# Four tiles of attention: the values product turned round, and one add of the weight decoding moved from GpSimd to VectorE

## The chip, the cores and the metric

The kernel runs on one core of a Trainium2 chip. The metric is the device time of one execution in microseconds (us); the median of several runs counts. A core has five engines that take their instructions in order: TensorE (PE, with PEld for its weight loads), VectorE (DVE), ScalarE (ACT), GpSimd (POOL) and SyncE (SP), which here issues every DMA.

## What is computed

Attention that keeps the 32 largest scores of each row, over 4 batches of 8 heads, 576 tokens and 64 columns; then an MLP with h * cos(h); then eight experts, all of them applied to all 2304 tokens and weighted by a matrix P that is normalised by rows and columns eight times.

```python
scores = scale * q @ k.T
mask = scores >= kth_largest(scores, 32)
attn = exp(where(mask, scores, -1e9) - max)
attn = attn / (attn.sum(-1) + 1e-9)
x = (attn @ v) as [2304, 512]
h = x @ w_in            # [512, 2048]
x2 = (h * cos(h)) @ w_out
P = exp(x2 @ w_gate - max)   # 8 rounds of row and column normalising
out = sum over e of P[:, e] * (relu(x2 @ w1[e]) @ w2[e])
```

`w_in` and `w_out` come in float64, all else in float32.

## The kernel before, in words

Every instruction is noted by `put` (or `dma`) in program order with what it reads and writes. `Plan.issue` then simulates the engines with estimated costs and picks, per engine, the ready instruction of lowest priority number; the order that results is fixed in each engine's queue. The priorities depend on the class of work: first attention, first MLP, decode, attention, other MLP. On DVE the first MLP (0) goes ahead of decode (0.5), which goes ahead of the first attention (1); on POOL and ACT the first attention (0) goes ahead of decode (1).

**Decode** (`decode`, lines 314 to 333) turns 32 blocks of [128, 512] float64 weights into float32 and writes them to DRAM: one DMA in, a shift on DVE (line 324), four passes on ACT (325 to 328), a product on POOL (329), a mask on DVE (330), a product on POOL (331), the last add on POOL (332), and one DMA out. Its buffers are rings of four or five. The 16 blocks of `w_in` come first, then the 16 of `w_out`.

**The opening** handles the first 512 tokens in four tiles of 128, in float32 products. `attention_tile` goes over 8 heads in pairs. For each head `att_tile` makes the scores on PE (line 450, two halves, evicted by ACT at 456), finds the 32nd largest on DVE (`max` and `match_replace`, 458, 463, 464), takes the exponential on ACT (460), masks it and sums the rows in one DVE instruction (465), adds 1e-9 to the sums on POOL (467), takes the reciprocal on DVE (468) and scales the row by it on POOL (469). PE transposes the row in five pieces (474), ACT evicts them to `at_f` (478). In `attention_tile` the function `av` then multiplies, with the values stationary and the probabilities moving, into 64 partitions of the PSUM bank `ps_t` (529), and ACT copies that to half a chunk of `x_f` (533), which thus holds the features on the partitions.

`moe1_tile_a` multiplies `x_f` by the decoded `w_in` (629), chunk by chunk of `x_f`, in two alternating banks; `gate` makes h * cos(h) (587 to 596, POOL, DVE and ACT); PE transposes it (638) and ACT evicts it to `gT` (641). `moe1_tile_b` multiplies by the decoded `w_out` (654) in one bank, transposes (661) and splits x2 into two float32r parts (668, 669). The program order is tile 0, tile 1, MLP a of 0, tile 2, MLP a of 1, MLP b of 0, and so on.

**After the opening**, from x2 of the first 512 tokens on, `fill` runs the experts on them (mm3, lines 371 to 373) beside the attention of the other tokens (`attention`, whose values product is at 500 and 502). Buffers of `fill` take the place of the first tiles' (pool `fl` after `first`), those of `attention` the place of decode's (`att` after `dec`). The rest of the first MLP and the experts of the other tokens follow.

Of the kernel before, what the change touches and what calls it, by code (L numbers as in the profile page):

```python
# [24 lines left out]
# priorities per engine (lower first) of: attention of the first tokens, their first MLP,  # L25
# the decoding of weights, attention of the other tokens, the other MLP work
# [10 lines left out]
class Buf:  # L37
    """A tile that is allocated when the first instruction on it is issued."""
# [13 lines left out]
class View:  # L52
    """A slice of a Buf's first free dimension"""
# [17 lines left out]
class Plan:  # L71
    """Instructions are noted in program order with what they read and write; `issue` orders
    them per engine (greedy, by priority, on estimated costs) and then issues them."""
# [156 lines left out]
def fused_kernel(tc, kq, vv, w_in, w_out, w_gate, w1, w2, out, B=4):  # L230
    """Every product of two float32 operands a*b is carried by float32r parts:
    a = ah + al and b = bh + bl, each part exact in float32r, and
    ah*bh + ah*bl + al*bh accumulates in float32."""
# [7 lines left out]
    NMAX = 320  # queries of an attention product  # L241
    # the tokens' cut, in tiles of 128: those whose second MLP runs beside the attention, one half
    # of them at a time, those whose first product there goes by Winograd's scheme, the rest
# [42 lines left out]
    # PSUM, a bank each  # L286
# [27 lines left out]
    def decode(src, keep, part):  # L314
        """float64 bits to the nearest float32; what is under 2**-126 becomes zero.
        With h and l the high and low words, the float32 of sign, exponent and the 20 high
        mantissa bits comes from h alone (11 exponent bits to 8: the low 8, the top one of
        them flipped), and l, scaled by the exponent, is added to it."""
        raw, mag, sgn, low = d_raw(), d_mag(), d_sgn(), d_low()
        dma(lambda: raw.ap, lambda: src.bitcast(I32), 1 << 19, writes=[raw])  # L320
        hi = lambda dt: raw.ap.bitcast(dt).rearrange("p (n t) -> p n t", t=2)[:, :, 1]
        lo = lambda: raw.ap.bitcast(U32).rearrange("p (n t) -> p n t", t=2)[:, :, 0]
        magf = lambda: mag.ap.bitcast(F32)
        put("DVE", 335, lambda: V.tensor_scalar(mag.ap, hi(I32), 3, 0x40000000, op0=ALU.logical_shift_left, op1=ALU.bitwise_xor), [raw], [mag])
        put("ACT", 613, lambda: A_.activation(sgn.ap, hi(F32), AF.Identity, bias=cols.ap[:, 1:2]), [raw, cols], [sgn])
        put("ACT", 613, lambda: A_.activation(sgn.ap, sgn.ap, AF.Sign, bias=cols.ap[:, 2:3]), [sgn, cols], [sgn])
        put("ACT", 520, lambda: A_.activation(low.ap, lo(), AF.Copy, scale=2.0**-52), [raw], [low])
        put("ACT", 520, lambda: A_.activation(magf(), magf(), AF.Abs), [mag], [mag])
        put("POOL", 1225, lambda: G_.tensor_tensor(magf(), magf(), sgn.ap, op=ALU.mult), [mag, sgn], [mag])
        put("DVE", 335, lambda: V.tensor_scalar(sgn.ap.bitcast(I32), mag.ap, -8388608, None, op0=ALU.bitwise_and), [mag], [sgn])  # L330
        put("POOL", 1225, lambda: G_.tensor_tensor(low.ap, low.ap, sgn.ap, op=ALU.mult), [low, sgn], [low])
        put("POOL", 1225, lambda: G_.tensor_tensor(low.ap, magf(), low.ap, op=ALU.add), [mag, low], [low])
        dma(keep, lambda: low.ap, 1 << 18, [low], [part])
# [7 lines left out]
    def split_cols(hi, lo, raw, n=512, eng="POOL"):  # L341
        """raw, hi, lo: (buffer, view) pairs; eng takes the low parts"""
        (rb, rv), (hb, hv), (lb, lv) = raw, hi, lo
        put("ACT", act_ns(n), lambda: A_.activation(hv(), rv(), AF.Copy), [rb], [hb])  # L344
        e, f, c = ("POOL", G_, pool_ns(n)) if eng == "POOL" else ("DVE", V, dve_ns(n))
        put(e, c, lambda: f.tensor_tensor(lv(), rv(), hv().bitcast(F32), op=ALU.subtract), [rb, hb], [lb])  # L346

    # who takes the first MLP's low parts of weights, ranges of hs, low parts of gates
# [28 lines left out]
    def mm12(o, ob, ah, al, bh, bl, n, start, stop, bufs):  # L377
        """mm3 in two steps, of which only the second needs bl"""
# [30 lines left out]
    at_r = ring_of("first", 2, [128, 5, 128], F32, "at_f")  # L409
    xf_r = ring_of("first", 2, [128, 4, 128], F32, "x_f")  # L410
# [24 lines left out]
    def att_tile(stats, dests, plain=None):  # L435
        """stats: (stationary q buffer, first column, head), whose scores add up to the tile's
        128 rows. dests: (first row, rows, head, first token column) of the tile. plain: the
        tile's operands where it goes by float32 products."""
# [30 lines left out]
        put("POOL", 724, lambda: G_.tensor_scalar(ex.ap, ex.ap, mc(35), 0.0, op0=ALU.mult, op1=ALU.add), [ex, (m, 35, 36)], [ex])  # L469
        pt = lambda: ps_t.ap.rearrange("p (c t) -> p c t", c=4)  # L470
        for c0, c1, p in ((0, 4, 128), (4, 5, 64)):
# [8 lines left out]
            for r0, rn, hd, t0 in dests:  # L480
# [3 lines left out]
                if c0:  # L484
                    # the low parts of the last 64 keys lie below the high ones
# [7 lines left out]
                put("DVE", dve_ns(k), lambda hv=hv, sv=sv, lv=lv: V.tensor_tensor(lv(), sv(), hv().bitcast(F32), op=ALU.subtract), [ps_t, hi], [lo])  # L493

# [15 lines left out]
    def attention_tile(t):  # L510
        """Tokens t * 128.. of the first batch, all heads, in float32 products"""
        nonlocal work
        work = "first attention"
        x_f, q = xf_r(), qp_r()
        s0 = t * 128
        dma(lambda: q.ap, lambda: kq[0:H, 0:64, 1, s0 : s0 + 128].rearrange("h d s -> d h s"), 1 << 18, writes=[q], slow=True)
        for pr in range(H // 2):
# [3 lines left out]
            dma(lambda v=v: v.ap, lambda hs=hs: vv[hs].rearrange("h p c d -> p h c d"), 128 * 2560, writes=[v])  # L521
            for j in range(2):
                at_f = at_r()
                att_tile([], [], dict(q=q, k=k, at=at_f, h=2 * pr + j))

                def av(v=v, j=j, at_f=at_f):
                    for c in range(5):
                        p = 64 if c == 4 else 128
                        T_.matmul(ps_t.ap[:64, :128], v.ap[:p, j, c, :], at_f.ap[:p, c, :], start=c == 0, stop=c == 4)

                put("PE", 1100.0, av, [v, at_f], [ps_t])
                r = slice(64 * j, 64 * j + 64)
                put("ACT", act_ns(128, psum=True), lambda pr=pr, r=r: A_.activation(x_f.ap[r, pr, :], ps_t.ap[:64, :128], AF.Copy), [ps_t], [(x_f, pr, pr + 1)])
# [37 lines left out]
    def load_cols(src, h, l, c0, t0, n):  # L571
        """Columns t0.. of src [128, 4, NT] as parts, to columns c0.. of h and l"""
# [8 lines left out]
    def gate(hs, rr, n=1024):  # L581
        """rr = hs * cos(hs), n columns; hs, rr: (buffer interval, view) pairs"""
# [31 lines left out]
    def moe1_tile_a(t, x_f):  # L614
        """hs * cos(hs) of 128 tokens, transposed; float32 products with the tokens stationary"""
# [60 lines left out]
    class Part:  # L676
        """A block of tokens in the first MLP: where its x, h, y, gates and x2 are"""
# [10 lines left out]
        # of the sums that share a bank, the first matmul opens the group and the last closes it  # L688
# [61 lines left out]
    def keep_raw(xb, i0):  # L750
        """x2 in float32 to slots i0.. of xb"""
# [14 lines left out]
    def keep_parts(h2, l2):  # L766
        """x2 as parts"""
# [14 lines left out]
    def gates(v, vb, n, g_r, psum):  # L782
        """relu(v) as parts"""
# [5 lines left out]
    def fill(e, t0, h_ring):  # L789
        """Expert e on the four tiles from t0, whose x2 is in x2fh and x2fl, not yet weighted"""  # L790
# [63 lines left out]
    # The first product of the second MLP by Winograd's form of Strassen's scheme, exact in  # L854
    # real arithmetic: with W1^T in blocks A and x2^T in blocks B (rows of A: the halves of F;
    # columns of A, rows of B: the halves of the model dimension; columns of B: halves of the
    # tokens), seven products of blocks give the four blocks C of W1^T x2^T.
    #   S1 = A21 + A22, S2 = S1 - A11, S3 = A11 - A21, S4 = A12 - S2
    #   T1 = B12 - B11, T2 = B22 - T1, T3 = B22 - B12, T4 = B21 - T2
    #   U = A11 B11 + S2 T2, V = U + S3 T3, W = S1 T1  # L860
    #   C11 = A11 B11 + A12 B21, C12 = U + W + S4 B22, C21 = V + A22 T4, C22 = V + W
# [3 lines left out]
    def combine(x2, th, tl):  # L865
        """The right operands from x2's four row blocks, slots 0-3 the first half of the
        tokens, 4-7 the second"""
# [11 lines left out]
    def weight_mix(e, j, wa_r, mix_r):  # L879
        """The left operands for F's chunks j and j + 4, as (hi, lo) chunks of two each"""  # L880
# [18 lines left out]
    def mixed_first(A, th, tl, mix_r, g_r):  # L899
        """The parts of relu of two chunks of F by both halves of the tokens"""  # L900
# [84 lines left out]
    def sum_fill():  # L985
        """The weighted sums of what `fill` kept, a term a step"""
# [29 lines left out]
    # the first 512 tokens: a tile at a time, so that the tensor engine has work early  # L1016
# [16 lines left out]
    # beside the attention of the other batches: the second MLP of 1024 tokens  # L1033
# [12 lines left out]
    # the first MLP of the others, and their second  # L1046
# [78 lines left out]
```

## Time and profile before

| | us |
|---|---|
| median of 3 runs | 2483.45 (2482.08 to 2484.89) |
| span of the profiled execution | 2483.0 |
| PE busy in it | 2390.7 (96%) |
| VectorE busy | 1929.3 (78%) |
| ScalarE busy | 1261.6 (51%) |
| GpSimd busy | 1258.1 (51%) |

No time of the profiled execution is given but its span, which runs from its first instruction to the end of its last. Busy shares are means over stages with different limits; the stretches have to be read one by one. "Granted clock" is the share of TensorE's full clock that it was given.

### The profile page before, as it was taken

Reading aid. Unit: us, or ns where it says so; the run is one execution under the profiler, and the core shown is the slowest. Engines: PE = TensorE matmul, PEld = TensorE weight load, DVE = VectorE, ACT = ScalarE, POOL = GpSimd, SP = SyncE. Lnnn points to the kernel's source line nnn. Section 1 sums busy time; section 2 is a strip of 40 time slices with the busy share of each in tenths; the row PEclk is TensorE's granted clock in tenths of the full one; section 3 lists DMA queues with packets and bytes.
Section 4 is the critical chain, followed back from the end, with each engine's and each line's share of the span. In section 5 each row is a group of like instructions: output and inputs, shape, how many; then the busy total and the mean of one; then the engine's idle time right before and its main releaser. Section 6 shows DMA issues by size and latency. Waiting matters only on the chain.

```text
span 2483.0 us, 33670 instructions
## 1 busy us (share of the span) xinstructions
PE 2390.7 (96%) x11261; PEld 1866.3 (75%) x11261; DVE 1929.3 (78%) x3570; ACT 1261.6 (51%) x2430; POOL 1258.1 (51%) x1332
## 2 busy tenths in 40 slices
PE   6889999999999889999999999989999999999999
PEld 3444568888777767878778878867888888888887
DVE  8999559999999999999961567577667676666665
ACT  6786556666666776666543666552232232232221
POOL 6886257566666776665544120264334334453440
PEclk8679999999999999999999999999999999999999
DMA  8776664344334333333333432212223223111111
GB/s 266 228 219 187 198 202 146 100 118 119 113 118 124 95 91 99 119 114 100 92 112 118 136 103 64 69 39 59 85 77 98 81 81 95 46 48 38 34 39 43
DMA packets 156606, 267.81 MB, mean 108 GB/s; under 512 B 15680, under 2 KB 54176, under 8 KB 156432
## 3 DMA queue, kind: packets, MB, share of 16 engines
q1 hardware_dynamic: 156432, 265.66, 35.5%
q8 instruction: 88, 1.44, 0.3%
q14 instruction: 86, 0.70, 0.1%
HBM read 231.90 MB, written 33.70 MB: 107 GB/s over the span
## 4 chain that ended last, share of the span: by engine, by line
PE 56%; DVE 22%; POOL 3%; ACT 2%; issue 2%; DMA 1%; SPq 0%; POOLq 0%; ACTq 0%; DVEq 0%
PE y L371 8%; PE y L373 8%; PE y L372 8%; DVE wk L463 5%; DVE m L464 5%; DVE ex L465 3%; PE g L373 2%; PE g L371 2%; PE g L372 2%; DVE gl L786 2%; PE h L371 2%; PE h L373 2%; PE h L372 2%; DVE atl L493 1%; DVE m L458 1%
## 5 line engine op out<-in xcount | busy, mean ns | idle before, releaser
L346 POOL TENSOR_TENSOR wlo<-raw,whi 128x512 fp32r<-128x512 f32 x320 | 429.0, 1343 | 266.5 <-ACT whi L344 219.1
L464 DVE MAX8 m<-wk 128x8 f32<-128x576 f32 x432 | 317.2, 748 | 2.1
L344 ACT ACTIVATE whi<-raw 128x512 fp32r<-128x512 f32 x376 | 235.0, 627 | 122.9 <-PE y L373 32.1
L980 DVE SCALAR_TENSOR_TENSOR acc<-y,P,acc 128x512 f32<-128x512 f32 x280 | 209.0, 747 | 86.8 <-PE y L373 85.9
L463 DVE MATCH_REPLACE8 wk<-m,wk 128x576 f32<-128x576 f32 x288 | 213.4, 742 | 1.2
L371 PE MATMUL y<-whi,gh 128*128 128x512 f32 x512 | 206.0, 402 | 0.0
L373 PE MATMUL y<-whi,gl 128*128 128x512 f32 x512 | 201.1, 393 | 0.0
L372 PE MATMUL y<-wlo,gh 128*128 128x512 f32 x512 | 200.7, 392 | 0.0
L456 ACT ACTIVATE sc<-s 128x288 f32<-128x288 f32 x288 | 117.3, 407 | 120.9 <-DVE ex L465 60.2
L474 PE MATMUL t<-ident,ex 128*128 128x128 f32 (+1 forms) x720 | 136.5, 290 | 31.1 <-DVE atl L493 7.0
L474 PEld LDWEIGHTS t<-ident,ex 128*128 128x128 f32 (+1 forms) x720 | 87.2, 141 | 102.8 <-issue 21.1
L465 DVE SCALAR_TENSOR_TENSOR ex<-sc,m,ex 128x576 f32<-128x576 f32 x144 | 157.2, 1092 | 1.5
L371 PE MATMUL y<-gh,xh 128*128 128x512 f32 x362 | 141.5, 391 | 0.0
L373 PE MATMUL y<-gh,xl 128*128 128x512 f32 x362 | 141.1, 390 | 0.0
L372 PE MATMUL y<-gl,xh 128*128 128x512 f32 x362 | 141.1, 390 | 0.0
L469 POOL TENSOR_SCALAR ex<-ex,m 128x576 f32<-128x576 f32 x144 | 113.2, 786 | 47.0 <-DVE m L468 43.1
L460 ACT ACTIVATE ex<-sc,m 128x576 f32<-128x576 f32 x144 | 111.5, 774 | 39.0 <-POOL m L459 37.6
L458 DVE MAX8 m<-sc 128x8 f32<-128x576 f32 x144 | 106.9, 743 | 20.6 <-ACT sc L456 20.6
L492 ACT ACTIVATE ath<-t 128x512 fp32r<-128x512 f32 (+3 forms) x256 | 97.6, 394 | 46.2 <-PE t L474 41.4
L373 PEld LDWEIGHTS y<-whi,gl 128*128 128x128 f32 x512 | 96.1, 188 | 21.5
L371 PE MATMUL y<-gh,gh 128*128 128x512 f32 x278 | 109.1, 392 | 3.2 <-ACT gh L785 2.1
L346 POOL TENSOR_TENSOR cl<-raw,ch 128x512 fp32r<-128x512 f32 x32 | 43.4, 1365 | 132.9 <-ACT ch L344 132.9
(420 smaller groups left out, 7156.6 us busy)
## 6 DMA issues: line engine op xcount, KB each, us to landing
raw<-in_w_dram SPq DMA_DIRECT2D x384, 256.0 KB, 2.7
kq<-in_kq_dram SPq DMA_DIRECT2D x32, 576.0 KB, 4.1
wp<-win_d SPq DMA_DIRECT2D x32, 512.0 KB, 4.4
wp<-wout_d SPq DMA_DIRECT2D x32, 512.0 KB, 4.3
y_d<-st SPq DMA_DIRECT2D x64, 256.0 KB, 2.6
raw<-y_d SPq DMA_DIRECT2D x64, 256.0 KB, 2.7
raw<-win_d SPq DMA_DIRECT2D x48, 256.0 KB, 3.0
raw<-wout_d SPq DMA_DIRECT2D x48, 256.0 KB, 2.7
```

Source lines behind the costliest of these rows:

```text
L344: put("ACT", act_ns(n), lambda: A_.activation(hv(), rv(), AF.Copy), [rb], [hb])
L346: put(e, c, lambda: f.tensor_tensor(lv(), rv(), hv().bitcast(F32), op=ALU.subtract), [rb, hb], [lb])
L371: T_.matmul(o(), ah(), bh(), start=start, stop=False)
L372: T_.matmul(o(), ah(), bl(), start=False, stop=False)
L373: T_.matmul(o(), al(), bh(), start=False, stop=stop)
L456: put("ACT", act_ns(288, psum=True), lambda c=c: A_.activation(sc.ap[:, c], o(), AF.Copy), [ps_s], [(sc, c.start, c.stop)])
L458: put("DVE", 669, lambda: V.max(mc(0, 8), sc.ap), [sc], [(m, 0, 8)])
L463: put("DVE", 669, lambda r=r, src=src: V.match_replace(wk.ap, mc(8 * r, 8), src.ap, LOWEST), [src, (m, 8 * r, 8 * r + 8)], [wk])
L464: put("DVE", 669, lambda r=r: V.max(mc(8 * r + 8, 8), wk.ap), [wk], [(m, 8 * r + 8, 8 * r + 16)])
L465: put("DVE", 729, lambda: V.scalar_tensor_tensor(ex.ap, sc.ap, mc(31), ex.ap, op0=ALU.is_ge, op1=ALU.mult, accum_out=mc(33)), [sc, ex, (m, ...
L474: T_.transpose(pt()[:p, c - c0, :], ex.ap[:, c * 128 : c * 128 + p], ident.ap)
L980: put("DVE", 663, lambda y=y, av=av, pcol=pcol: V.scalar_tensor_tensor(av(), y.ap, pcol(), av(), op0=ALU.mult, op1=ALU.add), [y, P, a], [a])
```

## The change

Only the functions below change; comments and docstrings are also taken out, which moves no instruction. In decode the last add goes to DVE, at the planner's cost for that engine. In the first four tiles, line 469 is left out; the product puts the tokens on the output partitions, with the probabilities stationary and the values moving, each head in its own 64 columns of the bank `ps_g`; ACT's eviction to the new buffer `x_t` multiplies by the reciprocal of the row sums; after the eighth head four transposes and one eviction make `x_f`.

```diff
-        put("POOL", 1225, lambda: G_.tensor_tensor(low.ap, magf(), low.ap, op=ALU.add), [mag, low], [low])
+        put("DVE", dve_ns(512), lambda: V.tensor_tensor(low.ap, magf(), low.ap, op=ALU.add), [mag, low], [low])
...
+    xt_r = ring_of("first", 2, [128, 512], F32, "x_t")
...
-        put("POOL", 724, lambda: G_.tensor_scalar(ex.ap, ex.ap, mc(35), 0.0, op0=ALU.mult, op1=ALU.add), [ex, (m, 35, 36)], [ex])
+        if not plain:
+            put("POOL", 724, lambda: G_.tensor_scalar(ex.ap, ex.ap, mc(35), 0.0, op0=ALU.mult, op1=ALU.add), [ex, (m, 35, 36)], [ex])
...
+        return (m, 35, 36), lambda: mc(35)
...
-                at_f = at_r()
-                att_tile([], [], dict(q=q, k=k, at=at_f, h=2 * pr + j))
+                at_f, h = at_r(), 2 * pr + j
+                rb, rv = att_tile([], [], dict(q=q, k=k, at=at_f, h=h))
+                d = slice(h * 64, h * 64 + 64)
...
-                        T_.matmul(ps_t.ap[:64, :128], v.ap[:p, j, c, :], at_f.ap[:p, c, :], start=c == 0, stop=c == 4)
+                        T_.matmul(ps_g.ap[:, d], at_f.ap[:p, c, :], v.ap[:p, j, c, :], start=c == 0, stop=c == 4)
 
-                put("PE", 1100.0, av, [v, at_f], [ps_t])
-                r = slice(64 * j, 64 * j + 64)
-                put("ACT", act_ns(128, psum=True), lambda pr=pr, r=r: A_.activation(x_f.ap[r, pr, :], ps_t.ap[:64, :128], AF.Copy), [ps_t], [(x_f, pr, pr + 1)])
+                put("PE", 1100.0, av, [v, at_f], [(ps_g, h, h + 1)])
+                put("ACT", act_ns(64, psum=True, ap=True), lambda d=d, rv=rv: A_.activation(x_t.ap[:, d], ps_g.ap[:, d], AF.Copy, scale=rv()), [(ps_g, h, h + 1), rb], [(x_t, h, h + 1)])
+
+        def tr():
+            for c in range(4):
+                T_.transpose(ps_t.ap[:, c * 128 : c * 128 + 128], x_t.ap[:, c * 128 : c * 128 + 128], ident.ap)
+
+        put("PE", 436.0, tr, [x_t, ident], [ps_t])
+        put("ACT", act_ns(512, psum=True), lambda: A_.activation(x_f.ap, ps_t.ap.rearrange("p (c t) -> p c t", c=4), AF.Copy), [ps_t], [(x_f, c, c + 1) for c in range(4)])
```

## Rows read from the trace of the kernel before

**Rows 1.** The page, span in 40 slices of 62 us, tenths busy.
```profile
PE   6889999999999889999999999989999999999999
...
DVE  8999559999999999999961567577667676666665
...
PEclk8679999999999999999999999999999999999999
```

**Rows 2.** Table of stretches: from:to, length, busy us of each engine, granted clock, DMA.
```profile
20.00:200.00 180.00, 150.51 (x463) 74.54 (x463) 172.81 (x324) 136.99 (x260) 150.78 (x155) 0.77 0.73 227
200.00:344.00 144.00, 138.59 (x523) 69.60 (x523) 91.22 (x184) 76.87 (x143) 54.32 (x72) 0.96 0.62 200
...
400.00:800.00 400.00, 395.40 (x1995) 320.65 (x1994) 394.12 (x855) 248.53 (x527) 246.81 (x311) 1.00 0.39 117
800.00:950.00 150.00, 133.09 (x633) 105.86 (x631) 143.66 (x252) 110.51 (x195) 110.61 (x108) 0.98 0.32 95
```

**Rows 3.** Groups by line, 0 to 300 us: busy us, mean ns, idle before.
```profile
L332 POOL TENSOR_TENSOR d_low<-d_mag,d_low 128x512 f32<-128x512 f32 x32 | 43.8, 1368 | 1.4
...
L465 DVE SCALAR_TENSOR_TENSOR ex<-sc,m,ex 128x576 f32<-128x576 f32 x32 | 36.5, 1142 | 0.1
...
L330 DVE TENSOR_SCALAR d_sgn<-d_mag 128x512 int32<-128x512 int32 x32 | 26.9, 840 | 2.1 <-POOL d_mag L329 2.0
L469 POOL TENSOR_SCALAR ex<-ex,m 128x576 f32<-128x576 f32 x32 | 26.4, 825 | 12.1 <-DVE m L468 11.3 <-PE y L638 0.7
...
L324 DVE TENSOR_SCALAR d_mag<-d_raw 128x512 int32<-128x512 int32 x32 | 24.1, 753 | 3.1 <-POOL d_low L332 2.5 <-DMA d_raw<-in_w_in_dram 0.6
...
L596 DVE TENSOR_TENSOR rr<-rr,hs 128x512 f32<-128x512 f32 x12 | 11.4, 988 | 2.5 <-ACT rr L591 2.5
...
L533 ACT ACTIVATE x_f<-t 64x128 f32<-64x128 f32 x32 | 8.6, 268 | 22.6 <-PE t L529 22.2
```

**Rows 4.** Single lines, 0 to 345 us: duration ns min/median/max, first and last start.
```profile
L596 DVE TENSOR_TENSOR rr<-rr,hs x16: 679/692/1758, 113.8 to 314.6; 128x512 f32<-128x512 f32 x16
...
L330 DVE TENSOR_SCALAR d_sgn<-d_mag x32: 401/752/1484, 18.3 to 208.1; 128x512 int32<-128x512 int32 x32
...
L324 DVE TENSOR_SCALAR d_mag<-d_raw x32: 402/596/1486, 12.0 to 188.7; 128x512 int32<-128x512 int32 x32
...
L465 DVE SCALAR_TENSOR_TENSOR ex<-sc,m,ex x33: 793/809/1869, 18.6 to 330.2; 128x576 f32<-128x576 f32 x33
```

**Rows 5.** Timeline, end of the opening: start us, length us, instructions.
```profile
284.86 0.08 DVE L465 DVE_READ_ACCUMULATOR ex<-sc,m,ex 128x1 f32 x1
...
294.25 1.45 PE L529 MATMUL t<-at_f,vp 128*64 128x128 f32 x10
...
304.46 1.88 PE L629 MATMUL h<-wp,x_f 128*128 128x512 f32 x4
...
309.36 5.42 PE L654 MATMUL y<-wp,gT 128*128 128x512 f32 x12 [0.21 <-DMA wp<-wout_d]
...
315.47 1.20 ACT L641 ACTIVATE gT<-y 128x512 f32<-128x512 f32 x2 [1.47 <-PE y L638]
...
343.81 0.44 PE L371 MATMUL g<-x2fh,whi 128*128 128x512 f32 x1
```

**Rows 6.** Timeline of PE's weight loads in a later values product.
```profile
344.91 0.19 PEld L502 LDWEIGHTS t<-atl,vs 128*128 128x128 f32 x1
345.02 0.19 PEld L500 LDWEIGHTS t<-ath,vs 128*128 128x128 f32 x1
```

**Rows 7.** Single lines, 0 to 345 us, columns as in rows 4.
```profile
L629 PE MATMUL y<-wp,x_f x64: 592/592/1221, 42.4 to 304.0; 128*128 128x512 f32 x64
...
L654 PE MATMUL y<-wp,gT x128: 592/592/1221, 193.9 to 339.9; 128*128 128x512 f32 x128
...
L332 POOL TENSOR_TENSOR d_low<-d_mag,d_low x32: 1264/1272/2378, 20.9 to 211.0; 128x512 f32<-128x512 f32 x32
```

**Rows 8.** Waits of DVE, 0 to 300 us: us in total, times, longest.
```profile
DVE m L468 <- POOL m L467: 5.1, 2, 4.1
```

More of the change, by code (lines that the diff above doesn't have):

```diff
@@ L513, in attention_tile @@
         work = "first attention"
-        x_f, q = xf_r(), qp_r()
+        x_f, x_t, q = xf_r(), xt_r(), qp_r()
         s0 = t * 128
@@ L520, in attention_tile, with av @@
             dma(lambda k=k, hs=hs: k.ap, lambda hs=hs: kq[hs, 0:64, 0, :].rearrange("h d s -> d h s"), 512 * S, writes=[k], slow=True)
-            dma(lambda v=v: v.ap, lambda hs=hs: vv[hs].rearrange("h p c d -> p h c d"), 128 * 2560, writes=[v])
+            dma(lambda v=v, hs=hs: v.ap, lambda hs=hs: vv[hs].rearrange("h p c d -> p h c d"), 128 * 2560, writes=[v])
             for j in range(2):
-                at_f = at_r()
-                att_tile([], [], dict(q=q, k=k, at=at_f, h=2 * pr + j))
-                def av(v=v, j=j, at_f=at_f):
+                at_f, h = at_r(), 2 * pr + j
+                rb, rv = att_tile([], [], dict(q=q, k=k, at=at_f, h=h))
+                d = slice(h * 64, h * 64 + 64)
+                def av(v=v, j=j, at_f=at_f, d=d):
                     for c in range(5):
                         p = 64 if c == 4 else 128
-                        T_.matmul(ps_t.ap[:64, :128], v.ap[:p, j, c, :], at_f.ap[:p, c, :], start=c == 0, stop=c == 4)
-                put("PE", 1100.0, av, [v, at_f], [ps_t])
-                r = slice(64 * j, 64 * j + 64)
-                put("ACT", act_ns(128, psum=True), lambda pr=pr, r=r: A_.activation(x_f.ap[r, pr, :], ps_t.ap[:64, :128], AF.Copy), [ps_t], [(x_f, pr, pr + 1)])
+                        T_.matmul(ps_g.ap[:, d], at_f.ap[:p, c, :], v.ap[:p, j, c, :], start=c == 0, stop=c == 4)
[6 more added lines that the diff above has]
+        put("ACT", act_ns(512, psum=True), lambda: A_.activation(x_f.ap, ps_t.ap.rearrange("p (c t) -> p c t", c=4), AF.Copy), [ps_t], [(x_f, c, c + 1) for c in range(4)])
         work = "mlp"
```

## The prediction

> **What bounds the kernel now.** I read the slices of the span first [rows 1]. PE reads 8 or 9 tenths in nearly every slice after the first, so an engine's total decides little here; what counts is where PE loses time. It loses most in the first six slices, where its granted clock also reads below 9 (8, 6, 7, 9), while VectorE (DVE) reads 9 or 8 from slice 2 to slice 4. The table of stretches says how much [rows 2]: from 20 to 200 us DVE is busy 172.8 of 180 us, and PE 150.5 us at a mean clock of 0.77, that is, a good part of its work runs at the lower level, 1.2 GHz. From 200 to 344 us PE is busy 138.6 of 144 us at 0.96 and DVE has room. So the opening is bound by DVE first and by PE's backlog afterwards. From 400 to 800 us both are full (PE 395.4, DVE 394.1 of 400). The first product of the second MLP starts at 343.81 us; call that F. After F PE stays nearly full, so I take the end of the kernel to move with F, one for one, as long as PE has work ready.
>
> **The change, part by part.** It has two edits, both in that opening.
>
> Edit 1, decode's last add. It removes 32 GpSimd (POOL) adds of 128x512, a mean 1368 ns each, 43.8 us [rows 3], and puts 32 adds with two SBUF inputs on DVE. Before shows no such add of decode on DVE; the nearest row is the gate's product at line 596, also 128x512 with two SBUF inputs, in the same stretch: 679 ns at least, 692 median, 988 mean [rows 3, 4]. The bounds are 32 x 0.679 = 21.7 us and 32 x 0.988 = 31.6 us; I take 0.75, 24 us, nearer to the lower end because POOL will have less to do. The output DMA of each block now waits for DVE in place of POOL; the number of DMAs is the same.
>
> Edit 2, the first attention. It removes 32 normalising passes on POOL, 26.4 us [rows 3], and the step "sum, reciprocal, normalise" leaves the way to the transposes: they can start when line 465 is done. The values product now loads the probabilities (128 columns) and streams the values (64 columns). Ten of its matmuls take 1.45 us today [rows 5]. Loads of 128 columns with 64 streamed stand at line 500/502, 0.11 us from one to the next [rows 6], so ten give about 1.1 us and the switch to the last, 64-row chunk what it costs today: I put the product at no change, with 1.1 to 1.8 us as bounds (32 x -0.35 to 32 x +0.35, -11 to +11 us of PE time; in the DVE-bound part DVE hides either). The eviction shrinks to 64 columns but gains a scale from SBUF: the old one took 268 ns [rows 3], I put the new at the same, in ACT's slack. Each tile adds four transposes and one 128x512 eviction; they lie on the way to the tile's first MLP, about 1.5 us, and are counted in the chain below.
>
> What edit 2 loses: x_f used to become readable pair by pair, and line 629 read it so: its first matmul ran at 42.4 us [rows 7], long before tile 0 was through. Now no chunk is readable before all eight heads are done. For tiles 0 to 2 the wait is covered by the next tile's attention. For tile 3 it is on the path.
>
> *Sum A, DVE's end of the first attention (284.94 us now, the last line 465 [rows 5]).* Adds: +24. Relief: DVE's operations that meet POOL vary widely. Line 330 has 401 ns as its least and 840 as its mean, line 324 402 and 753, line 465 793 and 1142 [rows 3, 4]; 32 x (0.439 + 0.351 + 0.349) = 36.4 us of DVE's time is spent blocked. By the kernel's code the opening has 144 long POOL operations (96 of decode, 32 normalising, 16 of gates); the change leaves 80, 44% fewer. In proportion that gives back 16 us; if decode just runs denser, nothing. I take 12. DVE's waits for POOL before the reciprocal, 5.1 us in all [rows 8], shrink by 3. A = +24 - 12 - 3 = +9 us, with bounds 21.7 - 16 - 5 = 0 and +31.6.
>
> The Trainium skill speaks against edit 1 here: its page "SBUF — State Buffer" (section "Who interferes with whom") says that a VectorE instruction with two SBUF inputs contends with a GpSimd one that reads SBUF, and that the loser blocks fully. The trace agrees: line 596 ranges from 679 to 1758 ns [rows 4]. By that rule at its worst each add would wait for a whole POOL add, and the 32 would cost about 60 us in place of 24 (an estimate); the mean of 988 ns says that most do not.
>
> *Sum B, from that end to F (58.9 us now, 343.81 - 284.94 [rows 5]).* Today PE's backlog fills it: line 654 of tile 0 could only start at 193.9 us [rows 7], since decode's last block is added at 211.0 us [rows 7], and so the second product of tile 2 still stands in front of that of tile 3. With 70 us of POOL's work gone decode should be through near 150 us, and line 654 of tile 0, 32 matmuls of 0.45 us (12 in 5.42 [rows 5]), 14.5 us, moves into the part where PE has room. What is left if nothing queues: about 6 us for the last head and the new transposes (an estimate from the 1.45 us product, two evictions of 0.6 and the hops between); line 629 in full, 14.5; the gate, from the end of line 629 to the last gT, 316.67 - 306.34 = 10.3; the second half of line 654, 16 x 0.45 = 7.2; the tail to F, 343.81 - 340.5 = 3.3 [rows 5, 7]. That is 41.3, or 17.6 us less than now. Some backlog will stay; I take B = -16, bounds -17.6 and 0.
>
> Together F moves by 9 - 16 = -7 us. The profiled execution has a span of 2483.0 us; no other time of it is shown, and the median of the runs is 2483.45, so the two stand 0.4 us apart and I apply the sum to the span: 2476.0 us.
>
> **The rivals.**
> 1. *Slower: the adds land on the full engine and the backlog stays.* The place is DVE from 20 to 285 us; the price 21.7 to 31.6 us for the adds, with relief of 0 to 12. It decides if decode in front of the attention pushes the heads back so far that the MLP of tiles 0 and 1, which now has to wait for whole tiles, meets a PE as full as today: then B is about 0 to -5. The time is 2483 + 10 to 2483 + 26, so 2493 to 2509. For it: DVE is busy 96% there. Against it: DVE's room after 200 us and the shorter way from line 465 to the transposes. Chance 0.26.
> 2. *No change: F moves, the end does not.* From 400 to 800 us DVE is as full as PE [rows 2]; if the attention of the second batch does not start earlier, PE only runs out of the first experts' work sooner and waits longer between 800 and 950 us, where it already loses 17 of 150 us [rows 2]. Or A and B cancel. The time is 2479 to 2488. Chance 0.25.
> 3. *Faster by more: relief in full.* A near +0.4 and B at -17.6 give -17: 2466. This is the lower end of "faster". Chance 0.10.
> 4. *It doesn't do what it says:* the product gets dearer by 0.35 us a head where PE is full (13 heads after 200 us), +4.5 us: 2480. It is inside rival 2's figures and has no chance of its own.
>
> **How the numbers follow.** The forecast (2470 to 2478.5) has 0.38, rival 3 has 0.10, rival 2 0.25, rival 1 0.26; 0.01 is left to anything else. A measurement can tell about 0.2%, 5 us, so faster (under 2478.5) is 0.48, same 0.25, slower 0.27. The range goes from 2465 to 2498: it leaves out a little of rival 3 and the upper half of rival 1. The range of the likeliest case alone is 2465 to 2479.
>
> **What would show it.** In the changed profile: POOL's line 332 gone and a DVE add of 128x512 there, mean 0.7 to 0.8 us; the means of lines 330, 324 and 465 down by some 0.1 us each; decode's last block near 150 us; line 654 starting before 170 us; the last line 465 of the first attention at about 294 us; F at about 337 us; the ten matmuls of a values product at 1.3 to 1.5 us. I am wrong if F lies after 344 us (rival 1), if F lies before 340 us and the span is unchanged (rival 2), or if decode still ends near 210 us, since then B has no source.

## The result and the profile after

The changed kernel takes 2511.18 us (median of 4 runs, 2509.74 to 2516.63) against 2483.07 us beside it: a ratio of 1.0114, 95% interval 1.0101 to 1.0126, so about 28 us slower. The profiled execution, the slowest of the four, has a span of 2514.8 us, 31.8 us over that of before. Lines move down by one behind line 409, by two behind 469, and by ten behind `attention_tile`: 465 is now 466, 474 is 476, 529 is 533, 589 and 599 correspond, 629 is 639, 654 is 664.

The page, the 40 slices (of 63 us now), answers to [rows 1]:

```profile
PE   5589999999999989999999999989999999999999
...
DVE  8996818999999999999971466668767666566665
...
PEclk9977999999999999999999999999999999999999
```

PE reads 5, 5 in the first two slices where it read 6, 8: what it lacks, it lacks at the very start. The table of stretches, for [rows 2]:

```profile
20.00:200.00 180.00, 126.75 (x373) 75.59 (x374) 176.51 (x330) 130.86 (x249) 117.45 (x112) 0.89 0.66 212
200.00:344.00 144.00, 143.67 (x537) 78.59 (x538) 91.66 (x195) 72.59 (x134) 19.12 (x39) 0.92 0.58 178
400.00:800.00 400.00, 394.91 (x2005) 320.94 (x2004) 388.85 (x847) 250.45 (x536) 252.79 (x316) 1.00 0.40 122
800.00:950.00 150.00, 137.74 (x665) 108.50 (x664) 147.94 (x278) 112.14 (x200) 115.20 (x118) 1.00 0.35 106
```

From 20 to 200 us PE is busy 126.8 us in place of 150.5, while DVE stays as full as it was. From 200 to 344 us PE is full, 143.7 of 144 us. POOL has given up 33 us of work before 200 us, and PE gets its work no sooner for it. The clock column of the first row can't be compared with that of before; the last section says why.

The first product of the second MLP (F), the last mask of the first attention, and the first products of the first MLP, from the timeline and from single lines (duration min/median/max, first and last start), for [rows 5, 7]:

```profile
310.87 0.08 DVE L466 DVE_READ_ACCUMULATOR ex<-sc,m,ex 128x1 f32 x1
...
371.39 0.44 PE L371 MATMUL g<-x2fh,whi 128*128 128x512 f32 x1
...
L639 PE MATMUL y<-wp,x_f x64: 592/592/1221, 121.1 to 330.8; 128*128 128x512 f32 x64
...
L664 PE MATMUL y<-wp,gT x128: 592/592/697, 239.5 to 367.4; 128*128 128x512 f32 x128
```

F is 27.6 us later (371.39 against 343.81) and holds nearly all of the loss. The first attention ends 26.0 us later (310.95 against 284.94); the way from there to F is 60.4 us, where it was 58.9. The products of tile 0 are late: the first one starts at 121.1 us for 42.4 (it can no longer start pair by pair) and ends at 155.9 for 131.2, and the second starts at 239.5 us for 193.9, though decode is done much earlier: its last add begins at 153.0 us, where it was 211.0 (single line, columns as above):

```profile
L332 DVE TENSOR_TENSOR d_low<-d_mag,d_low x32: 666/1153/1752, 22.0 to 153.0; 128x512 f32<-128x512 f32 x32
```

The groups by line up to 330 us, for [rows 3]:

```profile
L332 DVE TENSOR_TENSOR d_low<-d_mag,d_low 128x512 f32<-128x512 f32 x32 | 37.5, 1171 | 1.1 <-POOL d_low L331 1.1
L466 DVE SCALAR_TENSOR_TENSOR ex<-sc,m,ex 128x576 f32<-128x576 f32 x32 | 28.8, 902 | 0.1
...
L324 DVE TENSOR_SCALAR d_mag<-d_raw 128x512 int32<-128x512 int32 x32 | 19.4, 614 | 1.0 <-DMA d_raw<-in_w_in_dram 1.0
L330 DVE TENSOR_SCALAR d_sgn<-d_mag 128x512 int32<-128x512 int32 x32 | 17.9, 561 | 0.8 <-POOL d_mag L329 0.8
```

The add takes 1171 ns on DVE, nearly the 1368 it took on POOL. The other three got shorter together by 36.5 + 24.1 + 26.9 - 28.8 - 19.4 - 17.9 = 21.4 us. DVE's bill for these lines is 16.1 us higher.

How far the heads are by 153 us, when the last block of decode is added, shows the order in DVE's queue (masks begun before 153 us; before first, after below):

```profile
L465 DVE SCALAR_TENSOR_TENSOR ex<-sc,m,ex x15: 793/809/1829, 18.6 to 146.5; 128x576 f32<-128x576 f32 x15
```

```profile
L466 DVE SCALAR_TENSOR_TENSOR ex<-sc,m,ex x11: 804/805/1816, 19.8 to 146.9; 128x576 f32<-128x576 f32 x11
```

Fifteen heads against eleven. Later PE has fallen behind DVE, and DVE stands still in front of a gate (timeline of DVE; in brackets the idle time and its releaser):

```profile
208.84 0.74 DVE L464 MATCH_REPLACE8 wk<-m,wk 128x576 f32<-128x576 f32 x1
228.52 1.22 DVE L599 TENSOR_TENSOR rr<-rr,hs 128x1024 f32<-128x1024 f32 x1 [18.93 <-POOL rr L598]
229.66 0.81 DVE L466 SCALAR_TENSOR_TENSOR ex<-sc,m,ex 128x576 f32<-128x576 f32 x1
```

For 18.9 us DVE waits for tile 1's gate, whose input comes from PE by way of ACT and POOL. Masks of the next heads stand behind it in the queue. Up to the last mask of the first attention, DVE's waits of this kind made 3.4 us before and make 22.3 now (total, times, longest):

```profile
DVE rr L589 <- POOL rr L588: 3.4, 4, 1.6
```

```profile
DVE rr L599 <- POOL rr L598: 22.3, 4, 18.9
```

PE in the time of the long wait has all it can do and runs at 1.2 GHz (stretch 180 to 220 us, columns as above):

```profile
180.00:220.00 40.00, 39.02 (x97) 21.75 (x97) 29.58 (x69) 11.41 (x26) 1.90 (x10) 0.50 0.22 66
```

### The profile page after: what moved, and what is told of

Same layout as the page of the kernel before. It is cut to its first block, busy times and chain, and to the rows that moved or that the text cites. A ratio compares the mean times of both kernels' runs of the same rounds, so it can differ in the third digit from the quotient of the medians.

```text
span 2514.8 us, 33647 instructions
## 1 busy us (share of the span) xinstructions
PE 2399.8 (95%) x11277; PEld 1887.9 (75%) x11277; DVE 1939.4 (77%) x3602; ACT 1264.5 (50%) x2434; POOL 1195.0 (48%) x1268
## 4 chain that ended last, share of the span: by engine, by line
PE 66%; DVE 26%; POOL 3%; issue 2%; ACT 2%; DMA 1%; SPq 0%; POOLq 0%; ACTq 0%; DVEq 0%
PE y L371 9%; PE y L373 9%; PE y L372 9%; DVE wk L464 5%; DVE m L465 5%; DVE ex L466 3%; PE g L373 2%; PE g L372 2%; PE g L371 2%; PE h L371 2%; PE y L664 2%; PE h L373 2%; PE h L372 2%; PE t L476 2%; DVE m L459 2%
## 5 line engine op out<-in xcount | busy, mean ns | idle before, releaser
L466 DVE SCALAR_TENSOR_TENSOR ex<-sc,m,ex 128x576 f32<-128x576 f32 x144 | 151.1, 1049 | 1.3
L371 PEld LDWEIGHTS y<-whi,gh 128*128 128x128 f32 x512 | 96.7, 189 | 17.6
L373 PE MATMUL y<-gh,gl 128*128 128x512 f32 x278 | 108.5, 390 | 1.1 <-DVE gl L796 1.1
```

Source lines behind the costliest of these rows:

```text
L371: T_.matmul(o(), ah(), bh(), start=start, stop=False)
L373: T_.matmul(o(), al(), bh(), start=False, stop=stop)
L466: put("DVE", 729, lambda: V.scalar_tensor_tensor(ex.ap, sc.ap, mc(31), ex.ap, op0=ALU.is_ge, op1=ALU.mult, accum_out=mc(33)), [sc, ex, (m, ...
```

## The experiments

Two theories at first. *Adds*: the loss comes from edit 1, 32 more operations on the full VectorE. *Whole x_f*: it comes from edit 2, since the first MLP must wait for all eight heads. All ratios are to the kernel before, run beside it on the same chip.

**Edit 1 alone.**

```diff
-        put("POOL", 1225, lambda: G_.tensor_tensor(low.ap, magf(), low.ap, op=ALU.add), [mag, low], [low])
+        put("DVE", dve_ns(512), lambda: V.tensor_tensor(low.ap, magf(), low.ap, op=ALU.add), [mag, low], [low])
```

> Edit 1 alone on the kernel before: decode's last add on VectorE, the attention untouched. Theory 'adds': the loss comes from 32 more operations on a full VectorE, put ahead of the heads; then this run is slow too, 2500 to 2515 us. Theory 'whole x_f': the loss comes from the first MLP having to wait for all eight heads; then this run is within 6 us of 2483. If both are needed, 2485 to 2500.

2517.17 us, ratio 1.0136 (1.0119 to 1.0153), 2 us above what "adds" had expected. The whole loss and more is here.

**Edit 2 alone**: the changed kernel with the add back on POOL (the same line, reversed).

> Edit 2 alone: the changed attention, decode's last add back on GpSimd. Theory 'adds': 2470 to 2483 us, since the normalising pass is gone and nothing was put on VectorE. Theory 'whole x_f': 2500 to 2515 us, with the first x_f product (y<-wp,x_f) of tile 0 after its eighth head and TensorE idle before it. If both are needed, 2485 to 2500.

2480.26 us, ratio 0.9984 (0.9975 to 0.9994): a little faster than before. The two effects add up: +33 and -4 make +29, and both together measured +28. "Whole x_f" falls, at least as the cause. The traces do not take the same way, though. With edit 1 alone F is 18.2 us later and not 27.6, DVE waits 4.1 us for the gates' line 589 up to the last mask and not 22.3, and the profiled run takes 11.5 us longer behind F than that of before; what happens there was not traced.

**The changed kernel with x_f made pair by pair**, and **edit 2 alone in the same form**:

```diff
-        def tr():
-            for c in range(4):
-                T_.transpose(ps_t.ap[:, c * 128 : c * 128 + 128], x_t.ap[:, c * 128 : c * 128 + 128], ident.ap)
...
+            def tr(pr=pr):
+                T_.transpose(ps_t.ap[:, 0:128], x_t.ap[:, pr * 128 : pr * 128 + 128], ident.ap)
+
+            put("PE", 109.0, tr, [(x_t, 2 * pr, 2 * pr + 2), ident], [ps_t])
+            put("ACT", act_ns(128, psum=True), lambda pr=pr: A_.activation(x_f.ap[:, pr, :], ps_t.ap[:, 0:128], AF.Copy), [ps_t], [(x_f, pr, pr + 1)])
```

> The changed kernel, but each pair of heads is transposed and evicted to its own chunk of x_f at once, so the first MLP can start pair by pair as before. Theory 'whole x_f': 2480 to 2492 us, most of the 28 us come back. Theory 'adds': 2503 to 2515 us, since VectorE's order is nearly the same and the heads are as late as in the changed kernel (32nd mask at about 310 us).

2501.97 us, ratio 1.0076 (1.0061 to 1.0091): 1 us under what "adds" had expected, and far from "whole x_f".

> Edit 2 alone with the transposes by pairs: no add on VectorE, and x_f readable pair by pair. Both theories: not slower than before; 2465 to 2484 us. It would be the version that keeps what edit 2 takes from GpSimd without either suspected loss.

2491.71 us, ratio 1.0032 (1.0020 to 1.0044). Neither theory had this one. Pairs give back 9 us where PE starves (with edit 1), and cost 11 us where it doesn't: the last mask begins at 284.1 us with pairs and at 272.6 us without. With pairs, early products of x_f stand between the heads in PE's queue, two matmuls of 2.08 us together at 48.84 us; that these are what costs the 11 us is a guess that no run shows.

So edit 1 it is. But why 28 us in the changed kernel, when DVE's lines rose by 16? Edit 1 also changes the plan: the planner had decode at 3 x 1225 ns of POOL a block and now has 2 x 1225, so blocks come ready faster, and on DVE decode goes ahead of heads. *Time*: the adds' own time is the cost. *Order*: decode, no longer held back by POOL in the plan, is put ahead of the heads.

**The add cut to one column**, in the same order:

```diff
-        put("DVE", dve_ns(512), lambda: V.tensor_tensor(low.ap, magf(), low.ap, op=ALU.add), [mag, low], [low])
+        put("DVE", dve_ns(512), lambda: V.tensor_tensor(low.ap[:, 0:1], magf()[:, 0:1], low.ap[:, 0:1], op=ALU.add), [mag, low], [low])
```

> The changed kernel in its own order, with decode's add on VectorE cut to one of its 512 columns (the other columns keep the scaled low words alone, so the weights are not the right ones). Every instruction stays where it was; some 0.6 to 1.1 us of VectorE's time goes from each of the 32 adds, 19 to 35 us. Theory 'time': what costs is the adds' own time on the full VectorE; then 2476 to 2488 us. Theory 'order': what costs is that decode, no longer held back by GpSimd in the planner's estimate, is put ahead of the heads; then most of the loss stays, 2498 to 2511 us.

2502.51 us, ratio 1.0068 (1.0046 to 1.0090). Most of the loss stays, as "order" said. But the run took less away than it meant to; the single line (min/median/max) shows it:

```profile
L332 DVE TENSOR_TENSOR d_low<-d_mag,d_low x32: 135/716/1217, 21.4 to 142.3; 128x1 f32<-128x1 f32 x32
```

An add of one column takes 135 ns when it is let through, and 716 ns in the median. The 32 still cost 22.7 us in place of 37.5. So 8.7 us of the loss go with 14.8 us of DVE time, and the rest of the adds' time is waiting that the column count doesn't touch. The timelines show what is waited for (start us, length us; the changed kernel first, then this one):

```profile
117.85 1.27 POOL L331 TENSOR_TENSOR d_low<-d_low,d_sgn 128x512 f32<-128x512 f32 x1
118.42 1.25 DVE L332 TENSOR_TENSOR d_low<-d_mag,d_low 128x512 f32<-128x512 f32 x1
```

```profile
115.22 1.27 POOL L331 TENSOR_TENSOR d_low<-d_low,d_sgn 128x512 f32<-128x512 f32 x1
115.79 0.72 DVE L332 TENSOR_TENSOR d_low<-d_mag,d_low 128x1 f32<-128x1 f32 x1
```

An add that starts while a product of decode runs on POOL ends only after that product: 0.55 us after it with 512 columns (25 of the 32 adds, 547 to 553 ns), 0.02 us after it with one (26 of 32).

**The plan held back, the work unchanged**: the changed kernel with decode's two POOL products planned at 1838 ns each.

```diff
-        put("POOL", 1225, lambda: G_.tensor_tensor(magf(), magf(), sgn.ap, op=ALU.mult), [mag, sgn], [mag])
+        put("POOL", 1838, lambda: G_.tensor_tensor(magf(), magf(), sgn.ap, op=ALU.mult), [mag, sgn], [mag])
...
-        put("POOL", 1225, lambda: G_.tensor_tensor(low.ap, low.ap, sgn.ap, op=ALU.mult), [low, sgn], [low])
+        put("POOL", 1838, lambda: G_.tensor_tensor(low.ap, low.ap, sgn.ap, op=ALU.mult), [low, sgn], [low])
```

> The changed kernel with the planner told 1838 ns for each of decode's two GpSimd products, so that a block of decode costs GpSimd 3676 ns in the plan, as before (3 x 1225); the instructions are the same, only their order changes. Theory 'order': 2480 to 2492 us, the heads of tile 0 through by about 85 us in place of 110. Theory 'time': 2503 to 2515 us.

2490.19 us, ratio 1.0021 (1.0011 to 1.0030). Not one instruction was removed and 21 of the 28 us are gone. What stays against edit 2 alone, 2490.2 - 2480.3 = 10 us, is by difference what the adds cost in this order. The waits of DVE for line 598, up to 350 us (total, times, longest; the changed kernel first, then this one), show the stall shrunk:

```profile
DVE rr L599 <- POOL rr L598: 32.5, 6, 18.9
```

```profile
DVE rr L599 <- POOL rr L598: 13.6, 6, 8.2
```

Up to the end of its last mask DVE is now idle for 21.7 us, where the changed kernel had 39.9 (stretches up to that moment, the changed kernel first; DVE's busy time is the third):

```profile
0.00:310.94 310.94, 245.62 (x807) 140.41 (x807) 271.04 (x539) 200.51 (x379) 134.91 (x155) 0.90 0.63 197
```

```profile
0.00:284.74 284.74, 230.60 (x797) 134.72 (x797) 263.00 (x537) 199.10 (x378) 130.65 (x155) 0.90 0.68 213
```

So of the 26.2 us that the first attention ends earlier, 18.2 are DVE's idle time and 8.0 its busy time.

**The reverse**: edit 2 alone, the add on POOL, with all three POOL operations of decode planned at 817 ns in place of 1225, so that the plan runs decode as fast as the changed kernel's.

> Edit 2 alone (add on GpSimd) with the planner told 817 ns for each of decode's three GpSimd operations, 2451 ns a block, as the changed kernel's plan has it; the work is that of edit 2 alone, only the order changes. Theory 'order': slower than edit 2 alone by 15 to 30 us, 2495 to 2510. Theory 'time': 2475 to 2487 us.

2491.65 us, ratio 1.0025 (1.0015 to 1.0035): 11 us slower than edit 2 alone with the same work, less than the 15 to 30 expected. It lies between the ranges of the two theories, of which "time" had expected no loss at all. With the add on POOL decode doesn't in fact run as fast as planned (its last block comes at 191.6 us, not 153), and the heads are pushed back by less: tile 0's last mask begins at 88.2 us, between 78.7 and 109.5. That the one is the reason of the other was not tested.

**More of the same, in both directions.** Edit 2 alone with the three operations planned at 1400 ns:

> Edit 2 alone with the planner told 1400 ns for each of decode's three GpSimd operations, about what they take beside VectorE. Theory 'order': decode is spread a little more, the heads come a little sooner, 2470 to 2480 us. Theory 'time': as edit 2 alone, 2477 to 2484 us.

2479.84 us, ratio 0.9978 (0.9969 to 0.9987), which fits both theories. The changed kernel with the two products planned at 2450:

> As e6, with 2450 ns for each of decode's two products in the plan (4900 a block): decode is spread further than before. Theory 'order': the heads of tile 0 are through near 80 us, and what stays of the loss is the adds' time: 2482 to 2492 us. If decode then ends too late for the second product of the first MLP, 2495 or more.

2491.65 us, ratio 1.0033 (1.0022 to 1.0044): no better than with 1838, though tile 0's heads are now through as early as with edit 2 alone (79.9 and 78.7 us). Some 11 us remain against that run, and DVE is busy 12.1 us longer up to its last mask (263.7 and 251.6 us). The two agree in size, so I put this rest down to the adds' time; with the order of edit 2 alone it was not tried. Edit 2 alone with 1700:

> Edit 2 alone with 1700 ns planned for each of decode's three GpSimd operations, over what they take (1.32 to 1.49 us). Theory 'order': more heads before decode; 2472 to 2482 us. If decode's end (about 210 us with 1400 ns) moves out so far that the second product of the first MLP waits for it, 2484 us or more.

2479.23 us, ratio 0.9977 (0.9965 to 0.9989).

**The clock.** In the changed kernel PE runs at 1.2 GHz when its work arrives late. Is that a cost of its own? Behind each head of tiles 0 and 1 four matmuls that nobody needs were added, at the lowest priority:

```diff
+                if t < 2:
+                    work = "decode"
+                    for _ in range(4):
+                        put("PE", 4 * mm_ns(512), lambda v=v: T_.matmul(ps_y[3].ap, ident.ap, v.ap.rearrange("p a c d -> p (a c d)")[:, 0:512], start=True, stop=True), [v, ident], [ps_y[3]])
+                    work = "first attention"
```

> The changed kernel with four added float32 matmuls of 512 columns behind each head of tiles 0 and 1, at the lowest priority, into the bank y3 that nothing reads by then (64 matmuls, 128 in the trace, 28 us of TensorE at full clock, work that is not needed). In the changed kernel TensorE runs at 1.2 GHz until 138 us and again from 159 to 224 us. Theory 'clock': the low clock after the sparse start is part of the loss; with more work in the gaps the full clock is granted earlier, the stretch from 180 to 220 us reads over 0.8 in place of 0.50, and the time falls to 2490 to 2505 us. Theory 'late heads': the clock only follows; the time stays at 2508 to 2535 us, the added work coming on top where TensorE is full.

2509.77 us, ratio 1.0100 (1.0085 to 1.0114). The stretches of this run:

```profile
140.00:180.00 40.00, 35.81 (x137) 18.95 (x136) 36.62 (x69) 30.69 (x55) 26.17 (x28) 1.00 0.60 179
180.00:220.00 40.00, 40.00 (x162) 21.90 (x162) 36.17 (x84) 18.84 (x43) 6.05 (x16) 1.00 0.35 102
```

The full clock is there from 140 us, as "clock" expected, and DVE is busy 36.2 us between 180 and 220 in place of 29.6; F comes at 360.4 us, 11 earlier. The time is what "late heads" expected: 1.4 us under the changed kernel's median, intervals overlapping. In the profiled runs 5.6 us of the 11 reach the end of the span. So the clock is a link of the chain in the opening, but lifting it in this way brought nothing that could be told from no change. The added matmuls are work too, so what a full clock without them would give is not shown. Where the rest was given back after F was not traced.

**Half tiles.** Edit 2 alone with x_f made after heads 4 and 8:

```diff
+            if pr % 2:
+                def tr(pr=pr):
+                    for c in range(2):
+                        T_.transpose(ps_t.ap[:, c * 128 : c * 128 + 128], x_t.ap[:, (pr - 1 + c) * 128 : (pr + c) * 128], ident.ap)
...
```

> Edit 2 alone, but x_f made in two halves, after heads 4 and 8, in place of one (2480 us) or four (2492 us). If early products of x_f stand in front of the heads in TensorE's queue and slow them, the time lies between, 2482 to 2490 us; if half a tile is a better moment, 2470 to 2479 us.

2480.54 us, ratio 0.9983 (0.9974 to 0.9992): the same as once a tile, and neither of the two expected. Halves also put early products of x_f between the heads (the first at 56.0 us) and cost nothing, which speaks against the guess on the pairs above. Why pairs cost 11 us stays open.

The runs side by side (from the traces: start of the last mask of tile 0 and of the first attention, F; and the median), in us:

| kernel | tile 0 | attention | F | median |
|---|---|---|---|---|
| before | 77.7 | 284.1 | 343.8 | 2483.1 |
| changed | 109.5 | 310.1 | 371.4 | 2511.2 |
| edit 1 alone | 109.7 | 302.5 | 362.0 | 2517.2 |
| edit 2 alone | 78.7 | 272.6 | 335.1 | 2480.3 |
| changed, one column | 100.3 | 292.6 | 352.8 | 2502.5 |
| changed, planned at 1838 | 89.2 | 283.9 | 347.7 | 2490.2 |
| changed, planned at 2450 | 79.9 | 286.8 | 345.1 | 2491.7 |
| changed, by pairs | 104.5 | 297.4 | 355.2 | 2502.0 |
| changed, added matmuls | 109.7 | 300.1 | 360.4 | 2509.8 |
| edit 2, planned at 817 | 88.2 | 285.9 | 346.5 | 2491.7 |
| edit 2, planned at 1400 | 75.1 | 273.9 | 339.5 | 2479.8 |
| edit 2, planned at 1700 | 70.6 | 258.4 | 333.6 | 2479.2 |
| edit 2, by pairs | 78.9 | 284.1 | 341.0 | 2491.7 |
| edit 2, by halves | 78.5 | 276.2 | 334.0 | 2480.5 |

On the whole F and the time follow the moment at which tile 0's eight heads are through. It is no law: five kernels have it between 77.7 and 79.9 us, and their medians lie 11 us apart; and edit 1 alone has F 9 us before the changed kernel's and the longer time. Edit 2 without edit 1, planned at 1225, 1400 or 1700 ns, beats both kernels: the intervals of all three lie below 1, by 4 to 5 us against the kernel before.

## Why the prediction was wrong

I forecast 2476 us, faster with 0.48; it came out at 2511, past the range's 2498. The rival that came nearest was number 1, the adds on the full engine, with 0.26 and 2493 to 2509. Half of its mechanism came: decode in front of the attention pushes the heads back, and the MLP of tiles 0 and 1 meets a full PE. The other half did not. Its wait for whole tiles is not needed, since edit 1 alone loses as much without it, and its price was the adds' own time, where the plan alone returned 21 of the 28 us. Its upper end was also added up too low: by its own terms (31.6 for the adds, no relief, B at 0) it reaches 2515.

Two steps failed, by about as much: sum B by 17.6 us and sum A by 17.0.

*Sum B* I put at -16 us, and it measured +1.6 (60.4 against 58.9). The premise held: decode's last block came at 153.0 us, "near 150". The conclusion, that line 654 of tile 0 then moves before 170 us, did not: it started at 239.5. I took decode's end as what that line waits for. The traces show another thing in front of it, tile 1's whole first product, in PE's queue and, by the kernel's code, in the ring of four buffers `wp` that holds the weights of both products in program order (the changed kernel, then the one before; start us, length us):

```profile
172.79 1.06 ACT L651 ACTIVATE gT<-y 128x512 f32<-128x512 f32 x2
225.63 0.36 SPq L265 DMA_DIRECT2D wp<-win_d  x1
229.73 2.05 SPq L265 DMA_DIRECT2D wp<-wout_d  x2
235.25 1.02 PE L639 MATMUL h<-wp,x_f 128*128 128x512 f32 x2
239.54 1.98 PE L664 MATMUL y<-wp,gT 128*128 128x512 f32 x4
```

```profile
186.78 2.84 PE L629 MATMUL h<-wp,x_f 128*128 128x512 f32 x6
193.94 1.88 PE L654 MATMUL y<-wp,gT 128*128 128x512 f32 x4
```

Tile 0's gates were ready (gT) at 173.9 us and decode at 153.7; the line came 66 us behind the later of the two. In all fourteen kernels it starts within 5 us of the end of tile 1's first product, wherever decode ends. Five of them (us):

| kernel | decode's last add begins | tile 1's first product ends | second product of tile 0 starts |
|---|---|---|---|
| before | 211.0 | 189.6 | 193.9 |
| changed | 153.0 | 236.3 | 239.5 |
| edit 2 alone | 194.3 | 205.8 | 206.4 |
| changed, planned at 2450 | 226.1 | 197.0 | 196.8 |
| edit 2, planned at 1700 | 227.7 | 175.3 | 175.1 |

Tile 1's first product needs tile 1's heads, and these had paid for decode's haste: DVE, full in both kernels, ran the decode that was ready first, by the priorities that the front part quotes (0.5 ahead of 1). What POOL's slowness had done before, unnoticed, was to hold decode back and let heads through. Edit 1 took that brake away in the plan; the plan alone, put back, returned 21 us. Nor was the floor of 41.3 us in reach: the second product of tile 2 stood right in front of tile 3's, from 334.6 to 350.9 us, as it had from 306.2 to 322.9, and in no kernel of this case is B below 56 us.

*Sum A* was forecast at +9 and measured +26.0, inside its bounds of 0 to 31.6 but far from the value taken. DVE's busy and idle time up to the end of its last mask (before; that of the changed kernel stands above) shows where it came from:

```profile
0.00:284.93 284.93, 241.78 (x796) 119.22 (x797) 259.64 (x507) 200.14 (x376) 193.82 (x218) 0.84 0.71 220
```

DVE is 11.4 us longer busy (271.0 for 259.6) and 14.6 us longer idle (39.9 for 25.3). The busy part is near the +9 by two errors that cancel: the adds cost 37.5 us, not 24, and beyond the upper bound of 31.6, which came from a mean of operations a third of which ran after decode, with POOL quieter; and the relief was 21.4 us, not 12, since three lines got shorter by more than I took (other operations, the gates' products above all, give back some 5 us more). The idle part is a wait that no term had: DVE waits 18.9 us more for the gates' line 599, whose input had been there in time before and now came late from PE, while its other waits, those for the reciprocal among them, got 4.3 us shorter.

*The page of the Trainium skill*, "SBUF — State Buffer" (section "Who interferes with whom"), had spoken against edit 1: a VectorE instruction with two SBUF inputs contends with a GpSimd one that reads SBUF, and the loser blocks fully. This case's trace agrees better than I allowed: the add's least is 666 ns, its mean 1171, with one column 135 and 708, and 25 of the 32 adds end 0.55 us after the product on POOL that they met. The forecast by its worst, 60 us, was too much; the 24 I took was too little.

*The rest of edit 2.* The values product was put at no change: ten matmuls take 1.47 us at full clock (at 227.18 us), as 1.45 before; the 1.1 us taken from line 500/502 as a lower bound did not come. The eviction takes 307 ns, not 268; PE's transposes wait for it 0.9 us in all. That a whole x_f costs something was half right: it costs 9 us when the heads are late and saves 11 when they are on time. Edit 2 alone brought 3 to 4 us, much less than its F, 8.7 us earlier, would say by my rule of one for one; the rule holds only roughly. The slices of [rows 1] show PE and its clock below 9 in the first three, not in the first six.

*Rivals 2, 3 and 4* did not come. The lesson of the chances: I wrote the mechanism down as a rival and then priced the forecast as if it could not touch sum B.

## What to carry to other kernels

Where a planner orders the work, moving an operation off a slow engine also changes the order on every other engine; ask what that slow engine had been holding back, and who is behind it in the full one's queue. The time of work that becomes ready earlier is worth nothing if it then goes ahead of what the next stage needs first. Before a line's late start is put down to one input, look at what stands in front of it in its own queue and in its buffers: here the second product came behind another tile's first one, in every kernel. A single full engine with in-order queues turns into a wait as soon as another falls behind it: price that wait, not only the busy time that is moved.

## What the runs showed of the hardware that was not expected

An add on one column waits as long as one on 512: 708 against 1171 ns in the mean, with leasts of 135 and 666, so some 0.5 us of each is waiting, whatever its size. What sets the wait is the product on POOL that it meets, as the timelines above show. POOL waits as well: 13 products of lines 329 and 331 start while an add runs, with over 0.5 us of it to come; they take 1.67 to 1.73 us, where the least is 1.26, and end 1.12 to 1.14 us after the add.

The granted clock of the page can't be read in the first stretch. The table gives 1.00 for the changed kernel from 20 to 140 us, but four transposes take 1.12 us there and 0.60 us later, where the clock is 1.00 as well; by their length PE ran at 1.2 GHz (the stretch, then the timeline of PE, the first in the stretch, the second after it):

```profile
20.00:140.00 120.00, 73.95 (x199) 43.20 (x199) 120.00 (x212) 92.79 (x175) 90.59 (x79) 1.00 0.76 248
...
81.86 1.12 PE L476 MATMUL t<-ident,ex 128*128 128x128 f32 x4 [6.98 <-DVE ex L466]
...
231.25 0.60 PE L476 MATMUL t<-ident,ex 128*128 128x128 f32 x4
```

The first of them also shows PE idle for 7 us for want of a mask. PE was busy 74.0 of 120 us in that stretch, and again read 0.50 from 180 to 220 us while it was busy 39 of 40 us.
